# One GpSimd form for the gated inputs, whole-chunk loads, and a new issue order in a gated linear recurrence kernel

## The chip, the core and the metric

The kernel runs on one core of a Trainium2 chip. The metric is the device time of one execution in microseconds (us). The core has a matrix engine (PE, with its weight loads listed apart as PEld), a vector engine (DVE), a scalar engine (ACT), GpSimd (POOL) and SyncE (SP); here SP issues nearly all transfers between DRAM and the on-chip memory SBUF, and 16 DMA engines carry them. Matrix results land in PSUM. Each engine works through its own instructions in order and waits for the others through semaphores.

## What is computed

The inputs x, r_gate and i_gate have shape (4, 6336, 256) in float32. A gated linear recurrence over time is followed by a gated linear unit with a causal convolution of five taps:

```python
log_a = 8.0 * sigmoid(r_gate) * log(clip(sigmoid(a_param), 1e-6, 1 - 1e-6))
a_t = exp(log_a)
x_gated = sqrt(max(1 - a_t * a_t, 1e-6)) * sigmoid(i_gate) * x
for t in range(S):
    h = a_t[:, t] * h + x_gated[:, t]
    y[:, t] = h
gate = sigmoid(sum_k conv_w[k] * y[:, t - 4 + k])
out = (gate * (y @ w_val)) @ w_out
```

Three arrays are read and one is written, 26 MB each.

## The kernel before

The 4 x 6336 tokens are laid end to end (25344 tokens) and cut into 28 chunks (`CHUNKS`, line 16): 256, 512, then 23 of 1024, then 512, 256, 256. A chunk of 1024 is the unit of most counts below; all chunks together are 24.75 such units. Within a chunk, halves of 512 tokens (`subs`) serve as the unit of the later steps. Tokens arrive with time spread over partitions and the 256 channels along the free axis; the recurrence needs channels on partitions and time along the free axis, so the data pass through PE transposes.

The steps of chunk c, by the names that the plan uses:

- `ldri`, `ldx` (lines 216 to 227, SP): load r and i into a slot of `ri` (3 slots, `NRI`), and x into a slot of `xr` (3 slots, `NX`). One transfer for each half chunk and array: 512 KB, in pieces of 4 KB.
- `tanh` (line 293, ACT): tanh of r/2 and i/2, in place.
- `srT` (PE, line 306), `exp` (ACT, line 316): transpose tanh(r/2), and take the exponential into `aring`, which is a_t.
- `e` (POOL, line 322): a_t squared, into `ering`.
- `sq` (ACT, line 368): half the square root of 1 - a_t squared, for up to three chunks in one instruction, written as bf16 over the same ring. ACT loads another function table before it and after it.
- `s1` (POOL, line 336): tanh(i/2) + 1. `u` (POOL, line 359; DVE, line 356, in chunks 0 to 3): that times x, into `uring` (4 slots) in bf16. Two neighbouring tokens of a partition are stored as a pair for each channel, so that a pair can be transposed as one 32-bit value.
- `nT` (PE, line 381): transposes the square roots back, pairs as 32-bit values. `xg` (DVE, line 388): the product of u and nT. `xgT` (PE, line 397): transposes the product, so that time runs along the free axis.
- `scan` (DVE, line 410): the recurrence, in order from chunk to chunk.
- `conv` (PE, line 422), `tg` (ACT, line 433), `val` (PE, line 441), `gv` (DVE, line 447), `out` (PE, line 457), `osbD` or `osbA` (copy out of PSUM by DVE, line 467, or ACT, line 469), `store` (SP, line 480): the gated linear unit and the stores, 512 tokens at a time.

The list `FORM` (line 18) picks one of three forms for `tanh`, `s1` and `u` in each chunk:

- **Form 1** (chunks 4 to 8 and 17 to 27): two `tanh` instructions, the one for i written as float32 in place; `s1` in float32; `u` reads its two inputs with the pair innermost, that is, jumping by 256 elements and back, and writes in order.
- **Form 2** (chunks 0 to 3, on DVE, and 9 to 12): one `tanh` for r and i, written as bf16; `s1` in bf16; `u` reads both inputs in order and writes every second element.
- **Form 3** (chunks 13 to 16): as form 2, but `s1` writes the pairs, and `u` reads x jumping.

The order of all instructions on all engines is the text `PLAN` (lines 34 to 120), written out by hand: one word for each step, chunk, half and PSUM bank. Each engine runs its own share of it in this order. SP too is one queue: a load that waits for its slot holds back the stores behind it, and a store that waits for its copy holds back the loads. A load of r waits until `srT` has read the slot's chunk before it (three chunks earlier), a load of i and of x until `u` has.

Of the kernel before, what the change touches and what calls it, by code (L numbers as in the profile page):

```python
# [8 lines left out]
P = 128  # L9
HP = 64  # L10
SUBN = 512
BANK = 512
# [5 lines left out]
FORM = [2, 2, 2, 2, 1, 1, 1, 1, 1, 2, 2, 2, 2, 3, 3, 3, 3, 1, 1, 1, 1, 1, 1, 1, 1, 1, 1, 1]  # L18
NRI = 3
NX = 3  # L20
# [16 lines left out]
nT.0.0.0 xg.0.0.-1 u.1.-1 xgT.0.0.1 xgT.0.1.0 ldri.3.-1 scan.0.0.-1 scan.0.1.-1 sq.1.1.-1 srT.2.0.1 u.2.-1 srT.2.1.0  # L37
conv.0.0.2 val.0.0.4 exp.2.0.-1 nT.1.0.6 xg.1.0.-1 ldri.4.-1 xgT.1.0.7 xgT.1.1.6 scan.1.0.-1 exp.2.1.-1 e.2.0.-1
scan.1.1.-1 tanh.3.-1 e.2.1.-1 ldri.5.-1 tg.0.0.-1 srT.3.0.1 srT.3.1.0 gv.0.0.-1 exp.3.0.-1 conv.1.0.2 exp.3.1.-1
e.3.0.-1 out.0.0.4 val.1.0.6 tanh.4.-1 osbD.0.0.-1 e.3.1.-1 store.0.0.-1 ldx.3.-1 sq.2.2.-1 srT.4.0.1 s1.4.-1  # L40
srT.4.1.0 ldx.4.-1 u.3.-1 ldx.5.-1 tanh.5.-1 nT.2.0.4 nT.2.1.5 xg.2.0.-1 u.4.-1 xg.2.1.-1 nT.3.0.4 ldri.6.-1 xgT.2.0.5
xg.3.0.-1 scan.2.0.-1 xgT.2.1.4 exp.4.0.-1 scan.2.1.-1 nT.3.1.5 s1.5.-1 exp.4.1.-1 srT.5.0.1 exp.5.0.-1 srT.5.1.0
xg.3.1.-1 ldri.7.-1 e.4.0.-1 exp.5.1.-1 xgT.3.0.1 xgT.3.1.4 scan.3.0.-1 tg.1.0.-1 u.5.-1 tanh.6.-1 conv.2.0.2
gv.1.0.-1 scan.3.1.-1 val.2.0.0 ldx.6.-1 out.1.0.6 tg.2.0.-1 e.4.1.-1 srT.6.0.5 osbD.1.0.-1 srT.6.1.4 tanh.7.-1
conv.2.1.2 ldri.8.-1 e.5.0.-1 gv.2.0.-1 out.2.0.0 e.5.1.-1 val.2.1.6 osbD.2.0.-1 tg.2.1.-1 exp.6.0.-1 s1.6.-1
gv.2.1.-1 conv.3.0.0 exp.6.1.-1 srT.7.0.2 store.1.0.-1 val.3.0.6 e.6.0.-1 tg.3.0.-1 srT.7.1.3 store.2.0.-1 exp.7.0.-1
gv.3.0.-1 conv.3.1.0 e.6.1.-1 exp.7.1.-1 ldx.7.-1 out.2.1.4 tg.3.1.-1 val.3.1.2 osbD.2.1.-1 u.6.-1 sq.4.3.-1 out.3.0.0
gv.3.1.-1 ldx.8.-1 osbD.3.0.-1 out.3.1.2 osbD.3.1.-1 store.2.1.-1 e.7.0.-1 store.3.0.-1 e.7.1.-1 ldri.9.-1 tanh.8.-1
nT.4.0.0 nT.4.1.1 xg.4.0.-1 nT.5.0.2 s1.7.-1 xg.4.1.-1 nT.5.1.3 nT.6.0.0 xg.5.0.-1 xgT.4.0.1 xg.5.1.-1 xgT.4.1.2
xg.6.0.-1 u.7.-1 xgT.5.0.3 scan.4.0.-1 xgT.5.1.4 nT.6.1.5 store.3.1.-1 srT.8.0.0 srT.8.1.6 exp.8.0.-1 xg.6.1.-1  # L50
ldx.9.-1 scan.4.1.-1 xgT.6.0.5 exp.8.1.-1 xgT.6.1.1 s1.8.-1 tanh.9.-1 scan.5.0.-1 ldri.10.-1 conv.4.0.6 e.8.0.-1
scan.5.1.-1 val.4.0.2 u.8.-1 tg.4.0.-1 srT.9.0.0 srT.9.1.6 exp.9.0.-1 gv.4.0.-1 exp.9.1.-1 ldx.10.-1 scan.6.0.-1
conv.4.1.2 e.8.1.-1 out.4.0.6 tg.4.1.-1 scan.6.1.-1 val.4.1.4 tanh.10.-1 ldri.11.-1 e.9.0.-1 conv.5.0.2 gv.4.1.-1
e.9.1.-1 osbD.4.0.-1 out.4.1.0 tg.5.0.-1 val.5.0.4 osbD.4.1.-1 s1.9.-1 sq.7.3.-1 srT.10.0.2 store.4.0.-1 gv.5.0.-1
conv.5.1.6 s1.10.-1 srT.10.1.3 store.4.1.-1 val.5.1.0 ldx.11.-1 out.5.0.4 u.9.-1 osbD.5.0.-1 store.5.0.-1 tg.5.1.-1
nT.7.0.4 nT.7.1.5 xg.7.0.-1 u.10.-1 xg.7.1.-1 ldri.12.-1 nT.8.0.4 exp.10.0.-1 xgT.7.0.5 gv.5.1.-1 conv.6.0.6
exp.10.1.-1 xg.8.0.-1 out.5.1.0 scan.7.0.-1 tg.6.0.-1 val.6.0.2 tanh.11.-1 e.10.0.-1 xgT.7.1.4 gv.6.0.-1 conv.6.1.6
ldri.13.-1 osbD.5.1.-1 nT.8.1.5 e.10.1.-1 val.6.1.2 xg.8.1.-1 tg.6.1.-1 out.6.0.0 scan.7.1.-1 s1.11.-1 tanh.12.-1
srT.11.0.5 srT.11.1.6 xgT.8.0.7 gv.6.1.-1 xgT.8.1.4 u.11.-1 store.5.1.-1 osbD.6.0.-1 conv.7.0.2 exp.11.0.-1
scan.8.0.-1 store.6.0.-1 out.6.1.0 tg.7.0.-1 srT.12.0.5 ldx.12.-1 exp.11.1.-1 val.7.0.2 osbD.6.1.-1 e.11.0.-1  # L60
exp.12.0.-1 nT.9.0.7 srT.12.1.6 gv.7.0.-1 conv.7.1.0 tanh.13.-1 store.6.1.-1 e.11.1.-1 xg.9.0.-1 out.7.0.2 scan.8.1.-1
ldri.14.-1 nT.9.1.7 e.12.0.-1 xg.9.1.-1 tg.7.1.-1 val.7.1.4 osbD.7.0.-1 s1.12.-1 exp.12.1.-1 srT.13.0.7 conv.8.0.0
gv.7.1.-1 exp.13.0.-1 srT.13.1.2 e.12.1.-1 tg.8.0.-1 val.8.0.4 store.7.0.-1 exp.13.1.-1 out.7.1.6 gv.8.0.-1 u.12.-1
ldx.13.-1 sq.10.3.-1 conv.8.1.0 osbD.7.1.-1 out.8.0.2 val.8.1.4 osbD.8.0.-1 store.7.1.-1 xgT.9.0.6 xgT.9.1.7 e.13.0.-1
scan.9.0.-1 store.8.0.-1 ldri.15.-1 e.13.1.-1 scan.9.1.-1 tg.8.1.-1 nT.10.0.2 nT.10.1.3 s1.13.-1 nT.11.0.6 xg.10.0.-1
nT.11.1.7 tanh.14.-1 xg.10.1.-1 conv.9.0.0 gv.8.1.-1 u.13.-1 xgT.10.0.2 xg.11.0.-1 xgT.10.1.3 ldx.14.-1 val.9.0.4
xg.11.1.-1 scan.10.0.-1 out.8.1.6 tg.9.0.-1 tanh.15.-1 ldx.15.-1 conv.9.1.0 gv.9.0.-1 s1.14.-1 srT.14.0.2 osbD.8.1.-1
val.9.1.4 ldri.16.-1 u.14.-1 scan.10.1.-1 srT.14.1.6 tg.9.1.-1 xgT.11.0.7 exp.14.0.-1 out.9.0.0 gv.9.1.-1 exp.14.1.-1
xgT.11.1.3 srT.15.0.2 osbD.9.0.-1 conv.10.0.4 exp.15.0.-1 e.14.0.-1 scan.11.0.-1 srT.15.1.0 tg.10.0.-1 nT.12.0.1
store.8.1.-1 nT.12.1.2 exp.15.1.-1 e.14.1.-1 val.10.0.4 store.9.0.-1 xg.12.0.-1 out.9.1.6 tanh.16.-1 xg.12.1.-1  # L70
gv.10.0.-1 ldri.17.-1 e.15.0.-1 conv.10.1.0 osbD.9.1.-1 out.10.0.4 e.15.1.-1 scan.11.1.-1 xgT.12.0.2 tg.10.1.-1
val.10.1.6 srT.16.0.0 s1.15.-1 sq.13.3.-1 xgT.12.1.1 gv.10.1.-1 srT.16.1.3 store.9.1.-1 osbD.10.0.-1 conv.11.0.6
s1.16.-1 scan.12.0.-1 ldx.16.-1 out.10.1.4 u.15.-1 osbD.10.1.-1 store.10.0.-1 scan.12.1.-1 val.11.0.4 tg.11.0.-1
store.10.1.-1 nT.13.0.2 ldx.17.-1 u.16.-1 xg.13.0.-1 nT.13.1.1 tanh.17.-1 nT.14.0.2 xg.13.1.-1 conv.11.1.6 gv.11.0.-1
xgT.13.0.1 xg.14.0.-1 ldri.18.-1 val.11.1.4 scan.13.0.-1 xgT.13.1.2 tg.11.1.-1 s1.17.-1 exp.16.0.-1 scan.13.1.-1
conv.12.0.6 exp.16.1.-1 e.16.0.-1 out.11.0.0 tg.12.0.-1 gv.11.1.-1 srT.17.0.3 ldri.19.-1 srT.17.1.2 exp.17.0.-1
e.16.1.-1 nT.14.1.6 osbD.11.0.-1 val.12.0.4 exp.17.1.-1 xg.14.1.-1 out.11.1.0 u.17.-1 gv.12.0.-1 tanh.18.-1
conv.12.1.2 osbD.11.1.-1 out.12.0.4 val.12.1.0 store.11.0.-1 osbD.12.0.-1 xgT.14.0.7 tg.12.1.-1 srT.18.0.6 e.17.0.-1
store.11.1.-1 scan.14.0.-1 srT.18.1.4 exp.18.0.-1 conv.13.0.2 store.12.0.-1 exp.18.1.-1 e.17.1.-1 xgT.14.1.5
gv.12.1.-1 nT.15.0.6 ldri.20.-1 tg.13.0.-1 nT.15.1.4 xg.15.0.-1 val.13.0.0 tanh.19.-1 e.18.0.-1 xg.15.1.-1 out.12.1.2  # L80
scan.14.1.-1 conv.13.1.6 e.18.1.-1 xgT.15.0.4 gv.13.0.-1 xgT.15.1.5 tg.13.1.-1 s1.18.-1 osbD.12.1.-1 ldx.18.-1
val.13.1.0 sq.16.3.-1 out.13.0.6 scan.15.0.-1 s1.19.-1 conv.14.0.2 store.12.1.-1 gv.13.1.-1 srT.19.0.4 ldx.19.-1
osbD.13.0.-1 out.13.1.0 u.18.-1 scan.15.1.-1 val.14.0.6 store.13.0.-1 tg.14.0.-1 osbD.13.1.-1 srT.19.1.5 ldx.20.-1
u.19.-1 nT.16.0.0 exp.19.0.-1 gv.14.0.-1 conv.14.1.2 tanh.20.-1 xg.16.0.-1 out.14.0.6 store.13.1.-1 val.14.1.0
osbD.14.0.-1 ldri.21.-1 nT.16.1.4 e.19.0.-1 nT.17.0.6 xg.16.1.-1 nT.17.1.7 tg.14.1.-1 xg.17.0.-1 srT.20.0.4 xg.17.1.-1
exp.19.1.-1 xgT.16.0.6 s1.20.-1 gv.14.1.-1 conv.15.0.2 exp.20.0.-1 scan.16.0.-1 srT.20.1.5 val.15.0.0 tg.15.0.-1
e.19.1.-1 store.14.0.-1 exp.20.1.-1 xgT.16.1.4 out.14.1.2 gv.15.0.-1 ldri.22.-1 u.20.-1 conv.15.1.6 tanh.21.-1
osbD.14.1.-1 out.15.0.0 scan.16.1.-1 val.15.1.2 xgT.17.0.5 osbD.15.0.-1 xgT.17.1.4 tg.15.1.-1 e.20.0.-1 scan.17.0.-1
srT.21.0.0 store.14.1.-1 conv.16.0.6 exp.21.0.-1 e.20.1.-1 store.15.0.-1 srT.21.1.1 tg.16.0.-1 gv.15.1.-1 nT.18.0.0
nT.18.1.5 ldri.23.-1 exp.21.1.-1 e.21.0.-1 xg.18.0.-1 val.16.0.2 xg.18.1.-1 tanh.22.-1 out.15.1.0 scan.17.1.-1  # L90
e.21.1.-1 conv.16.1.6 xgT.18.0.5 gv.16.0.-1 s1.21.-1 xgT.18.1.4 tg.16.1.-1 osbD.15.1.-1 val.16.1.2 ldx.21.-1
sq.19.3.-1 s1.22.-1 out.16.0.6 scan.18.0.-1 conv.17.0.0 store.15.1.-1 gv.16.1.-1 srT.22.0.5 osbD.16.0.-1 ldx.22.-1
val.17.0.2 u.21.-1 scan.18.1.-1 out.16.1.6 store.16.0.-1 tg.17.0.-1 osbD.16.1.-1 srT.22.1.4 ldx.23.-1 nT.19.0.6
u.22.-1 nT.19.1.7 tanh.23.-1 gv.17.0.-1 conv.17.1.0 xg.19.0.-1 out.17.0.2 store.16.1.-1 xg.19.1.-1 nT.20.0.6
# [48 lines left out]
def kernel(  # L143
# [60 lines left out]
    with tc.manual_schedule():  # L204
# [11 lines left out]
        def op_ldri(k, bank):  # L216
            c = k[0]
            for o, n in subs[c]:
                j0, j1 = o // P, (o + n) // P
                for e, src in ((0, rf), (1, if_)):  # L220
                    nc.sync.dma_start(ri[:, c % NRI, e, j0:j1, :], toks(src, c, o, n))  # L221
# [304 lines left out]
```

## Time and profile before

The time before is 348.25 us, the median of 3 runs (347.41 to 348.39). The profiled execution took 345.86 us, of which the span, from the first to the last recorded instruction, is 344.0 us.

| | before |
|---|---|
| median of the runs | 348.25 us |
| profiled execution | 345.86 us |
| its span | 344.0 us |
| bytes moved by the SP queue | 104.35 MB |
| granted TensorE clock, mean | 0.907 |
| last load issued | 296 us |
| last `u` ends on POOL | 312.5 us |

Two kinds of view carry the reading. The first page gives the busy time of each engine, as a sum and in 40 slices of 8.6 us, a digit being tenths of the slice. The view by stretches gives, for any stretch of the span, the busy time of each engine, the granted clock, the share of the DMA engines' time that was used, and what they moved. A share over the whole span says little here, because the first 40 us, the middle and the last 40 us have different limits.

### The profile page before, as it was taken

What the parts mean: (1) busy time and instruction counts of PE and PEld (TensorE: products, weight loads), DVE (VectorE), ACT (ScalarE), POOL (GpSimd) and SP (SyncE); (2) the same over time, 40 slices, a digit from 0 to 9 for tenths busy, and PEclk for the clock granted to TensorE, in tenths of its full rate; (3) what the DMA queues carried; (4) which work ended last, traced back from release to release, by engine and by line L of the source; (5) the groups of instructions that cost most, each with busy time, mean ns of one, the idle gap of its engine ahead of it and who ended that gap; (6) DMA issues with size and microseconds to landing.
All of it is one profiled execution on the core that took longest, in us unless ns stands there. A gap on an engine that the chain in (4) does not pass through costs nothing.

```text
span 344.0 us, 6490 instructions
## 1 busy us (share of the span) xinstructions
PE 258.7 (75%) x2591; PEld 175.1 (51%) x2591; DVE 256.7 (75%) x231; ACT 285.1 (83%) x206; POOL 276.3 (80%) x116
## 2 busy tenths in 40 slices
PE   1157477848576598969968996998479929799994
PEld 0144354548333366646646664765356614565562
DVE  3184478648771699799999998999459934699973
ACT  7999999977737999999999989999597919667553
POOL 1325399999999999899999999999999999952000
PEclk9996879967898899989999999999769976899998
DMA  8999899796798999999999999995999815332334
GB/s 286 370 394 382 338 372 361 242 416 240 272 317 283 362 363 354 403 381 403 381 358 386 392 374 378 324 361 178 368 365 347 345 64 202 136 126 109 138 124 183
DMA packets 30012, 104.76 MB, mean 305 GB/s; under 512 B 3351, under 2 KB 3870, under 8 KB 29982
## 3 DMA queue, kind: packets, MB, share of 16 engines
q1 hardware_dynamic: 29968, 104.35, 81.0%
q8 instruction: 20, 0.33, 0.4%
q14 instruction: 10, 0.08, 0.1%
q10 hardware_dynamic: 14, 0.01, 0.0%
HBM read 78.39 MB, written 25.95 MB: 303 GB/s over the span
## 4 chain that ended last, share of the span: by engine, by line
PE 24%; POOL 20%; DMA 19%; issue 16%; DVE 9%; ACT 7%; SPq 3%; DVEq 0%; POOLq 0%; ACTq 0%
POOL uring L359 12%; PE pp L422 8%; DMA ri<-in_i_gate_dram 7%; PE pp L457 6%; POOL ering L322 6%; PE pp L441 5%; DMA xr<-in_x_dram 5%; DMA ri<-in_r_gate_dram 4%; DVE yring L410 3%; DVE osb L467 3%; POOL ri L336 3%; PE pp L306 2%; ACT tg L433 2%; SPq L221 2%; PE pp L397 2%
## 5 line engine op out<-in xcount | busy, mean ns | idle before, releaser
L359 POOL TENSOR_TENSOR uring<-ri,xr 128x2048 bf16<-128x2048 f32 (+3 forms) x24 | 138.7, 5789 | 7.6 <-PE pp L381 5.0
L410 DVE TENSOR_TENSOR_SCAN yring<-aring,yring,pp 128x1024 bf16<-128x1024 f32 (+2 forms) x54 | 114.8, 2140 | 5.6 <-PE pp L397 4.1
L322 POOL TENSOR_TENSOR ering<-aring 128x1024 f32<-128x1024 f32 (+2 forms) x56 | 93.9, 1701 | 26.6 <-ACT aring L316 26.6
L447 DVE SCALAR_TENSOR_TENSOR gv<-tg,pp 128x1024 bf16<-128x1024 bf16 (+1 forms) x51 | 59.9, 1175 | 29.0 <-ACT tg L433 16.5
L422 PE MATMUL pp<-yring,diag 64*64 64x512 bf16 (+15 forms) x1196 | 72.1, 373 | 8.3 <-ACT tg L433 6.1
L316 ACT ACTIVATE aring<-pp,khf 128x1024 f32<-128x1024 bf16 (+2 forms) x56 | 59.8, 1112 | 5.7 <-PE pp L306 5.7
L441 PE MATMUL pp<-yring,wv 128*128 128x512 bf16 (+1 forms) x204 | 52.5, 380 | 12.9 <-ACT osb L469 6.8
L467 DVE COPY osb<-pp 128x1024 f32<-128x1024 f32 (+1 forms) x39 | 46.3, 1189 | 19.8 <-PE pp L457 17.4
L433 ACT ACTIVATE tg<-pp 128x1024 bf16<-128x1024 f32 (+1 forms) x51 | 51.0, 1000 | 12.0 <-PE pp L422 12.0
L457 PE MATMUL pp<-wo,gv 128*128 128x256 bf16 x396 | 54.4, 282 | 3.6 <-DVE gv L447 3.3
L381 PE MATMUL pp<-ident_f,ering 128*128 128x128 f32 x198 | 37.2, 332 | 25.8 <-ACT ering L368 14.4
L368 ACT ACTIVATE ering<-ering,b 128x4096 bf16<-128x4096 f32 (+4 forms) x16 | 46.7, 2934 | 10.9 <-POOL ering L322 10.7
L457 PEld LDWEIGHTS <-gv 128*128 128x128 bf16 x396 | 41.9, 116 | 21.4 <-DVE gv L447 8.5
L306 PE MATMUL pp<-ident_b,ri 128*128 128x128 bf16 x396 | 33.2, 235 | 22.0 <-ACT ri L301 10.7
L422 PEld LDWEIGHTS <-diag 64*64 64x64 bf16 x1196 | 31.9, 113 | 34.6 <-issue 21.0
L381 PEld LDWEIGHTS pp<-ident_f,ering 128*128 128x128 f32 x198 | 30.4, 211 | 30.9 <-ACT ering L368 15.5
L301 ACT ACTIVATE ri<-ri 128x4096 bf16<-128x4096 f32 (+2 forms) x12 | 39.1, 3261 | 8.1 <-DMA ri<-in_i_gate_dram 8.1
L336 POOL TENSOR_SCALAR ri<-ri 128x2048 f32<-128x2048 f32 (+3 forms) x24 | 44.6, 1870 | 1.0 <-ACT ri L299 1.0
L306 PEld LDWEIGHTS <-ri 128*128 128x128 bf16 x396 | 27.9, 106 | 31.3 <-ACT ri L301 16.6
L388 DVE TENSOR_TENSOR uring<-uring,pp 128x1024 bf16<-128x1024 bf16 (+1 forms) x51 | 33.0, 665 | 11.0 <-PE pp L381 9.5
L397 PE MATMUL pp<-ident_f,uring 128*128 128x128 f32 x198 | 33.7, 304 | 5.7 <-DVE uring L388 4.5
L299 ACT ACTIVATE ri<-ri 128x2048 f32<-128x2048 f32 (+2 forms) x16 | 27.2, 1699 | 9.2 <-DMA ri<-in_i_gate_dram 9.1
(37 smaller groups left out, 132.2 us busy)
## 6 DMA issues: line engine op xcount, KB each, us to landing
ri<-in_r_gate_dram SPq DMA_DIRECT2D x48, 512.0 KB, 7.1
ri<-in_i_gate_dram SPq DMA_DIRECT2D x48, 512.0 KB, 6.7
xr<-in_x_dram SPq DMA_DIRECT2D x48, 512.0 KB, 7.8
out_dram<-osb SPq DMA_DIRECT2D x48, 512.0 KB, 5.2
ri<-in_r_gate_dram SPq DMA_DIRECT2D x3, 256.0 KB, 3.5
ri<-in_i_gate_dram SPq DMA_DIRECT2D x3, 256.0 KB, 2.9
xr<-in_x_dram SPq DMA_DIRECT2D x3, 256.0 KB, 3.5
out_dram<-osb SPq DMA_DIRECT2D x3, 256.0 KB, 2.4
```

What stands on the lines that cost most here:

```text
L306: nc.tensor.transpose(out=ppb[:, bank * 2 * BANK + j * P:bank * 2 * BANK + (j + 1) * P], in_=tri[:, c % NRI, 0, j * D + h * P:j * D + (h + ...
L316: nc.scalar.activation(out=dst, in_=src, func=ACT.Exp, scale=khf[:, h:h + 1], bias=khf[:, h:h + 1])
L322: nc.gpsimd.tensor_tensor(out=ering[:, c % NE, h * n:(h + 1) * n], in0=a, in1=a, op=ALU.mult)
L359: nc.gpsimd.tensor_tensor(out=u, in0=t, in1=xt, op=ALU.mult)
L381: nc.tensor.transpose(out=pp[:, d0:d0 + P], in_=src[:, w, :], identity=ident_f[:])
L410: nc.vector.tensor_tensor_scan(out=yring[:, h, y0:y0 + n], data0=aring[:, c % NA, h, 0:n], data1=src, initial=prev, op0=ALU.mult, op1=ALU.add)
L422: nc.tensor.matmul(out=pp[col * HP:(col + 1) * HP, b0 + d0:b0 + d1], lhsT=diag[r * HP:(r + 1) * HP, h, kk, :], rhs=yring[r * HP:(r + 1) * ...
L433: nc.scalar.activation(out=tg[:, :, 0:n], in_=two(live["conv", k], n), func=ACT.Tanh, scale=0.5)
L441: nc.tensor.matmul(out=pp[:, (bank + m) * BANK:(bank + m) * BANK + n], lhsT=wv[:, hk, m, :], rhs=yring[:, hk, y0:y0 + n], start=(hk == 0), ...
L447: nc.vector.scalar_tensor_tensor(out=gv[:, :, 0:n], in0=live.pop(("tg", k))[:, :, 0:n], scalar=1.0, in1=two(live["val", k], n), op0=ALU.ad ...
L457: nc.tensor.matmul(out=pp[:, bank * BANK + j * D:bank * BANK + (j + 1) * D], lhsT=gv[:, m, 0:n].rearrange("c (p q) -> c q p", q=q)[:, j, : ...
L467: nc.vector.tensor_copy(out=osb[:, 0:w], in_=src)
```

## The change

There are three edits and a new order.

- `FORM` is gone. All chunks use form 2: one `tanh` that writes r and i as bf16, `s1` in bf16, and a `u` that reads in order and writes every second element. Chunks 0 to 3 keep their `u` on DVE.
- A load is one transfer for each array and chunk: 1 MB in pieces of 8 KB for a full chunk.
- With the whole-chunk load, partition p holds 8 neighbouring tokens rather than 4 of each half. The orders in which `exp`, `nT` and `xgT` read and write follow from it: `exp` reads PSUM over 8 blocks; `nT` reads `ering` with a step of 4 values of 32 bits (2 before); `xgT` writes PSUM with a step of 4 (2 before). Stores keep the half chunks and 4 KB pieces.
- `PLAN` is another order of the same 886 steps, from the 24th word on. There are as many steps of each kind as before, the `sq` groups hold the same chunks, and 12 copies are on ACT as before, some of them other ones.

```diff
-FORM = [2, 2, 2, 2, 1, 1, 1, 1, 1, 2, 2, 2, 2, 3, 3, 3, 3, 1, 1, 1, 1, 1, 1, 1, 1, 1, 1, 1]
...
         def op_ldri(k, bank):
             c = k[0]
-            for o, n in subs[c]:
-                j0, j1 = o // P, (o + n) // P
-                for e, src in ((0, rf), (1, if_)):
-                    nc.sync.dma_start(ri[:, c % NRI, e, j0:j1, :], toks(src, c, o, n))
+            for e, src in ((0, rf), (1, if_)):
+                nc.sync.dma_start(ri[:, c % NRI, e, 0:CHUNKS[c] // P, :], toks(src, c, 0, CHUNKS[c]))
 
         def op_ldx(k, bank):
             c = k[0]
-            for o, n in subs[c]:
-                j0, j1 = o // P, (o + n) // P
-                nc.sync.dma_start(xr[:, c % NX, j0:j1, :], toks(xf, c, o, n))
+            nc.sync.dma_start(xr[:, c % NX, 0:CHUNKS[c] // P, :], toks(xf, c, 0, CHUNKS[c]))
...
-            if FORM[c] == 1:
-                nc.scalar.activation(out=tri[:, c % NRI, 0, 0:w], in_=src[:, 0], func=ACT.Tanh, scale=0.5)
-                nc.scalar.activation(out=src[:, 1], in_=src[:, 1], func=ACT.Tanh, scale=0.5)
-                return
             nc.scalar.activation(out=tri[:, c % NRI, :, 0:w], in_=src, func=ACT.Tanh, scale=0.5)
...
-            q = subs[c][0][1] // P
-            src = ppb[:, b * 2 * BANK:b * 2 * BANK + n].rearrange("c (s q p) -> c s p q", p=P, q=q)
-            dst = aring[:, c % NA, h, 0:n].rearrange("c (s p q) -> c s p q", p=P, q=q)
+            src = ppb[:, b * 2 * BANK:b * 2 * BANK + n].rearrange("c (q p) -> c p q", p=P)
+            dst = aring[:, c % NA, h, 0:n].rearrange("c (p q) -> c p q", p=P)
...
+            t = tri[:, c % NRI, 1, 0:CHUNKS[c] * H]
+            nc.gpsimd.tensor_scalar(out=t, in0=t, scalar1=1.0, scalar2=1.0, op0=ALU.add, op1=ALU.mult)
...
+            u = uring[:, c % NU, 0:w].rearrange("p (w d b) -> p w b d", b=2, d=D)
+            t = tri[:, c % NRI, 1, 0:w].rearrange("p (w b d) -> p w b d", b=2, d=D)
+            xt = xr[:, c % NX, 0:w // D, :].rearrange("p (w b) d -> p w b d", b=2)
...
-                i0 = (h * CHUNKS[c] + o) // 2
-                src = ering[:, c % NE, i0:i0 + n // 2].rearrange("c (p w) -> c w p", w=nw)
-                for w in range(nw):
-                    d0 = bank * BANK + w * D + h * P
+                src = ering[:, c % NE, h * nch // 2:(h + 1) * nch // 2].rearrange("c (p w) -> c w p", p=P)
+                for w in range(w0, w1):
+                    d0 = bank * BANK + (w - w0) * D + h * P
                     nc.tensor.transpose(out=pp[:, d0:d0 + P], in_=src[:, w, :], identity=ident_f[:])
...
-            for o, n in subs[c]:
-                nw = n // (2 * P)
-                u = uring[:, c % NU, o * H:(o + n) * H].bitcast(FP32)
-                dst = pp[:, bank * BANK + o // 2:bank * BANK + (o + n) // 2].rearrange("c (p w) -> c w p", w=nw)
...
+            n = CHUNKS[c]
+            u = uring[:, c % NU, 0:n * H].bitcast(FP32)
+            dst = pp[:, bank * BANK:bank * BANK + n // 2].rearrange("c (p w) -> c w p", p=P)
+            for w in range(n // (2 * P)):
```

## The prediction

> **What bounds the kernel now.** I read the page first. Its busy sums are close together (columns: busy us, share of the span, instructions), so no engine's sum decides. The slices show where each is full.
>
> ```profile
> PE 258.7 (75%) x2591; PEld 175.1 (51%) x2591; DVE 256.7 (75%) x231; ACT 285.1 (83%) x206; POOL 276.3 (80%) x116
> ACT  7999999977737999999999989999597919667553
> POOL 1325399999999999899999999999999999952000
> DMA  8999899796798999999999999995999815332334
> ```
>
> POOL is full from 43 us to 300 us without a gap; ACT and DMA have holes in slices 8 to 12 and after 26. The view by stretches, cut at the `tanh` of chunks 9, 11, 22 and 24, shows what the holes mean (columns: stretch; length; busy us of PE, PEld, DVE, ACT, POOL with counts; granted clock; DMA share; GB/s).
>
> ```profile
> 2.00:87.00 85.00, 51.57 (x443) 37.85 (x443) 50.45 (x67) 76.87 (x56) 56.77 (x26) 0.86 0.93 349
> 87.00:121.00 34.00, 21.30 (x178) 12.49 (x175) 19.58 (x15) 24.09 (x14) 34.00 (x11) 0.85 0.86 307
> 121.00:234.00 113.00, 98.97 (x1104) 68.95 (x1105) 106.03 (x83) 109.02 (x71) 111.36 (x45) 0.98 1.00 374
> 234.00:265.00 31.00, 23.34 (x212) 15.74 (x208) 23.04 (x20) 23.98 (x18) 31.00 (x10) 0.83 0.84 311
> 265.00:303.00 38.00, 28.58 (x275) 17.59 (x268) 24.74 (x19) 26.28 (x25) 38.00 (x17) 0.82 0.49 183
> 303.00:344.00 41.00, 34.95 (x399) 22.44 (x397) 32.62 (x30) 24.43 (x27) 4.51 (x6) 0.97 0.36 142
> ```
>
> From 121 to 234 us everything is full: DMA 1.00, ACT 96.5% (109.0 of 113), DVE 94%. There a faster POOL buys nothing. From 87 to 121 and from 234 to 303, POOL alone is full. The chain of waits and ACT's timeline show how it holds the others up to the end: `u` of chunk 23 (L359) gives its slot back, only then is the load of i for chunk 26 issued, and ACT, in order, stands for it with `sq` of chunks 22 to 24 behind.
>
> ```profile
> 272.90 7.31 POOL uring L359
> 280.23 2.70 DMA ri<-in_i_gate_dram
> 283.01 0.63 ACT L299 ACTIVATE ri<-ri 128x512 f32<-128x512 f32 x1 [5.83 <-DMA ri<-in_i_gate_dram]
> ```
>
> SP's own waits say the same: 90.1 us in 17 waits of a load for `u`.
>
> ```profile
> SPq L221 <- POOL uring L359: 90.1, 17, 9.9
> ```
>
> **POOL's part of the change** has rows, since all three forms run now. By shape (columns: busy, mean ns | idle before), float32 is form 1, bf16 forms 2 and 3 together; the timeline tells these apart (171 and 176 us are form 3, 109 and 113 us form 2, two chunks each).
>
> ```profile
> L359 POOL TENSOR_TENSOR uring<-ri,xr 128x2048 bf16<-128x2048 f32 x13 | 96.8, 7453 | 5.2 <-PE pp L381 5.0
> L359 POOL TENSOR_TENSOR uring<-ri,xr 128x2048 bf16<-128x2048 bf16 x8 | 34.0, 4270 | 0.3
> ...
> L336 POOL TENSOR_SCALAR ri<-ri 128x2048 f32<-128x2048 f32 x13 | 24.7, 1907 | 1.0 <-ACT ri L299 1.0
> ```
>
> ```profile
> 109.67 3.78 POOL L336 TENSOR_SCALAR ri<-ri 128x2048 bf16<-128x2048 bf16 x2
> 113.39 8.20 POOL L359 TENSOR_TENSOR uring<-ri,xr 128x2048 bf16<-128x2048 bf16 x2
> 171.20 5.00 POOL L336 TENSOR_SCALAR ri<-ri 128x2048 bf16<-128x2048 bf16 x2
> 176.09 8.77 POOL L359 TENSOR_TENSOR uring<-ri,xr 128x2048 bf16<-128x2048 bf16 x2
> ```
>
> Form 2 costs 4.12 us for `u` (about half of 8.20) and 1.9 for `s1`, form 1 7.45 and 1.9, form 3 4.4 and 2.5. Going to form 2: 13 x (7.45 - 4.12) = 43.3; the three small chunks, scaled by the same ratio, 3.5 of 7.9; form 3, 4 x (0.3 + 0.6) = 3.6. POOL falls by 50 us, from 276 to about 226. It was full for some 260 us, so it is no longer the bound, and what this is worth is the slack of the next engines.
>
> **ACT.** Form 1's two `tanh` take 2 x 1.913 us, form 2's one 3.618: 13 x 0.21 = 2.7 us less. Against it, the one `tanh` waits for r and i, where r's half could run while i was in flight. L299 waited three times for i, so at most 3 x 1.9 = 5.7 us are lost, at least 0; waits of this kind shrink when slots come free earlier, and I take 0. `exp` with 8 blocks: its times for 256, 512 and 1024 elements are 564, 778 and 1212 ns, a constant slope, although the first has blocks of 2 and the others of 4. I take 0.
>
> **Transfers.** The same bytes, in 84 loads for 153, 69 issues of 0.45 us fewer on SP. SP is not the bound, for it spends its time in waits. Below, a coarser load can land a first half later; above, longer pieces can move more. I take 0. Two statements of the Trainium skill would alter the sum. "DMA: Bandwidth & Descriptors", Anatomy of one DMA, fits a fixed 2.0 us to each transfer (measured on GpSimd's path), and its Bandwidth section counsels 1 MB; 69 x 2.0 would be 138 us gained. That is for transfers one after another; here 512 KB transfers overlap, and 374 GB/s over 113 us at share 1.00 leave no such gaps. The other speaks against the change: its Specifications put HBM for one core at about 358 GB/s. The loads up to chunk 24 (23.75 units x 3.15 MB = 74.7 MB) and the stores of some 18.5 units (19.4 MB) are 94.1 MB; at 358 that is 263 us, and chunk 24's `tanh` is at 265 already: nothing would be left to gain before the tail. The row decides: 374 on average over the full stretch, and as a best stretch
>
> ```profile
> 149.00:161.00 12.00, 11.33 (x102) 8.07 (x103) 10.99 (x10) 11.97 (x8) 11.76 (x6) 0.86 1.02 407
> ```
>
> At 374, 94.1 MB take 252 us.
>
> **PE.** `nT`'s weight load reads every second 32-bit value; `xgT`'s reads in order. Between 186 and 200 us (min/median/max ns):
>
> ```profile
> L381 PEld LDWEIGHTS pp<-ident_f,ering x12: 194/209/216, 188.7 to 198.1; 128*128 128x128 f32 x12
> L397 PEld LDWEIGHTS pp<-ident_f,uring x8: 138/140/143, 194.0 to 197.2; 128*128 128x128 f32 x8
> ```
>
> The step of 2 costs 70 ns of load, yet the matmuls follow each other every 120 ns rather than 109, since loads overlap. The change makes it a step of 4, 16 bytes, for which no row exists. The Trainium skill ("SBUF — State Buffer", Door 1) says SBUF has lines of 16 bytes and needs two hits in a line for full speed; the step of 2 has two hits and was dearer all the same. By line counts (32, 64, 128 in a row of 128 values) the load would go to 140 + 3 x 70 = 350 ns. From the row alone `nT` gains 0; with the rule, a load hidden by half, the pace becomes some 190 ns: 190 transposes x 70 = 13 us of PE, spread over the span, of which I put 1.5 us on the path (in the full tail). `xgT`'s PSUM step doubles to 16 bytes; at 8 bytes it shows no price (109 ns against 120), so 0, at most a doubling to 220.
>
> **The order.** The same steps, so no busy time. I take 0; bound from both sides by 5 us, one of the waits seen (4 to 7 us at 261 to 295 us) gained or lost.
>
> **The sum.** Each stretch shrinks until DMA moves 374 GB/s or ACT is 96.5% busy, whichever takes longer.
> - 2 to 87: DMA 85 x 349/374 = 79.3, ACT 79.7: -5.3.
> - 87 to 121: DMA 34 x 307/374 = 27.9, ACT 25: -6.1.
> - 121 to 234: ACT's cheaper `tanh` only, DMA holds: -1.
> - 234 to 265: DMA 25.8, ACT 24.9: -5.2.
> - 265 to 303: loads no longer wait for `u`. PE at the 85% of the last stretch: 28.6/0.85 = 33.6; ACT 27.2: -4.4 to -10, I take -7.
> - 303 to 344: PE and DVE with their dependences, POOL idle: 0.
> - PE's dearer transposes: +1.5.
>
> Together -23: span 344 -> 321, execution 345.9 -> 323. The runs' median stood 2.4 us over the profiled execution (0.7%), so 325 by median.
>
> **Rivals.**
> - **A, the sum**: 325 (317 to 332). For it: the holes of ACT and DMA lie where POOL alone is full. 0.58.
> - **B, the hole was not POOL's alone**: DMA gives no more than 358, or SP's stores hold loads back instead (`store` waited 72 and 41 us for copies, 37 of it at the end). Then -2, -5, 0, -4 and -4.4: -15.4 + 1.5 = -14, median 334. Against it: 374 over 113 us. 0.18.
> - **C, PE's strides become the bound; slower.** PE is 258.7 busy and reached 88% in its fullest stretch. If the step of 4 takes both kinds of transposes to 300 ns, PE gains 198 x (180 + 191) = 73 us; 332 at 90% is a span of 369, median 373. It decides from 0.9 x 344 - 258.7 = 51 us on, that is, 129 ns more for each of 396 transposes. Against it: 70 ns of load for the step of 2 gave 11 ns of pace. 0.10.
> - **D, more**: 8 KB pieces move 400 GB/s and ACT packs to 99%: -7, -8, -5, -7, -10 = -37, median 311. 0.11.
> - **No change**: form 2 costs more in other company. Eight neighbours at 4.1 to 4.4 speak against it. 0.03.
>
> **Range and chances.** From D's edge to past B: 309 to 338; C is left out, and the far ends of D and B. A measurement of this kernel tells 0.3% (1 us) from no change. Faster: A, B, D, 0.87; same 0.03; slower 0.10.
>
> **What would show it.** `u` at 4.1 us in all chunks, POOL near 226 us with idle time before `u`; SP's wait for `u` far below 90 us; DMA share near 1.00 until chunk 24, whose `tanh` comes near 247 us; `nT`'s load at 209 to 350 ns. Wrong, if DMA's share stays under 0.95 although SP doesn't wait for POOL, if PE's pace in L381 or L397 passes 240 ns, or if waits for stores take POOL's place.

## The result, and the profile after

The changed kernel takes 321.14 us (median of 4 runs, 320.46 to 323.72) where the one before took 348.07 beside it: a ratio of 0.924, with a 95% interval of 0.919 to 0.930. The forecast was 325, with 309 to 338 around it. The profiled execution took 321.38 us, its span is 319.6. Medians and ratios, here and below, leave out executions in a slower state, more than 1.5% above the fastest of the same kernel.

The page of the kernel after, its busy sums and the slices of POOL, DMA and the granted clock (8 us each):

```profile
PE 246.9 (77%) x2591; PEld 171.1 (54%) x2591; DVE 257.7 (81%) x231; ACT 283.0 (89%) x190; POOL 227.4 (71%) x116
POOL 0215478996999969957997699995995999561000
PEclk9998958998999799998999999999999999999999
DMA  7999999099999979989999989999999897613343
GB/s 223 398 385 421 419 425 403 23 325 425 424 412 371 362 292 326 410 331 388 366 337 385 414 308 392 346 385 424 398 349 391 317 351 270 249 72 131 134 180 150
```

POOL fell from 276.3 to 227.4 us and now has gaps all along. ACT, with 89% of the span, is the fullest. One slice stands out, the eighth: 56 to 64 us, in which the DMA engines moved 23 GB/s. A second profile of the same kernel has the hole in the same slice, with 20 GB/s.

POOL's rows by shape (columns: busy, mean ns | idle before and what ended it), and SP's own waits:

```profile
L333 POOL TENSOR_TENSOR uring<-ri,xr 128x2048 bf16<-128x2048 bf16 x21 | 86.4, 4120 | 14.0 <-DMA xr<-in_x_dram 11.1 <-PE pp L370 2.5
L320 POOL TENSOR_SCALAR ri<-ri 128x2048 bf16<-128x2048 bf16 x21 | 39.7, 1902 | 7.1 <-ACT ri L292 7.1
```

```profile
SPq L453 <- DVE osb L440: 164.7, 37, 14.6
SPq L453 <- ACT osb L442: 33.8, 12, 5.0
SPq L218 <- PE pp L297: 14.4, 3, 7.9
SPq L218 <- POOL uring L333: 10.2, 5, 4.2
```

The waits of stores before:

```profile
SPq L480 <- DVE osb L467: 72.1, 25, 8.3
SPq L480 <- ACT osb L469: 41.4, 12, 7.3
```

`u` on POOL takes 4.12 us in every full chunk, and three times it waited for x, 11.1 us in all. SP's waits of loads of r and i for POOL's `u` shrank from 90.1 us to 10.2; those of stores for their copies grew from 72.1 + 41.4 to 164.7 + 33.8.

The view by stretches, cut at the `tanh` of the same chunks as the prediction (9, 11, 22, 24), so that the lengths of the rows can be laid beside it:

```profile
2.00:90.00 88.00, 49.85 (x459) 36.11 (x459) 52.17 (x67) 77.91 (x53) 55.48 (x29) 0.90 0.92 361
90.00:114.00 24.00, 17.76 (x170) 11.45 (x163) 18.83 (x15) 23.21 (x14) 23.41 (x10) 0.93 0.96 378
114.00:229.00 115.00, 101.77 (x1119) 70.94 (x1121) 108.78 (x85) 107.34 (x65) 98.07 (x46) 0.99 0.96 367
229.00:252.00 23.00, 18.95 (x194) 13.54 (x187) 21.00 (x18) 22.89 (x14) 19.74 (x10) 1.00 0.97 364
252.00:319.60 67.60, 58.61 (x663) 39.04 (x661) 56.72 (x48) 51.28 (x48) 30.02 (x20) 1.00 0.53 197
```

The total agrees with the sum, but the parts do not: the first stretch took 88 us where 79.7 were expected and 85 were taken before. The cut moves with the order, though: by the `tanh` of chunk 9 PE has done 459 matmuls here and 443 before. That asked for experiments which take form, loads and order apart.

### The profile page after: what moved, and what is told of

It reads as the page before. It is cut to its first block, busy times and chain, and to the rows that moved or that the text cites. A ratio compares the mean times of both kernels' runs of the same rounds, so it can differ in the third digit from the quotient of the medians.

```text
span 319.6 us, 6375 instructions
## 1 busy us (share of the span) xinstructions
PE 246.9 (77%) x2591; PEld 171.1 (54%) x2591; DVE 257.7 (81%) x231; ACT 283.0 (89%) x190; POOL 227.4 (71%) x116
## 4 chain that ended last, share of the span: by engine, by line
PE 21%; ACT 17%; POOL 15%; issue 14%; DVE 11%; DMA 11%; SPq 0%; POOLq 0%; DVEq 0%; ACTq 0%
DMA ri<-in_i_gate_dram 8%; PE pp L395 7%; POOL ering L312 6%; POOL uring L333 6%; DVE yring L383 5%; ACT ering L342 5%; PE pp L430 5%; PE pp L414 4%; ACT ri L292 4%; ACT tg L406 3%; DVE gv L420 3%; DMA xr<-in_x_dram 3%; DVE osb L440 2%; PE pp L355 2%; ACT L342 2%
## 5 line engine op out<-in xcount | busy, mean ns | idle before, releaser
L333 POOL TENSOR_TENSOR uring<-ri,xr 128x2048 bf16<-128x2048 bf16 (+2 forms) x24 | 90.8, 3792 | 14.1 <-DMA xr<-in_x_dram 11.1
L292 ACT ACTIVATE ri<-ri 128x4096 bf16<-128x4096 f32 (+2 forms) x28 | 90.1, 3223 | 7.2 <-DMA ri<-in_i_gate_dram 4.4
L395 PE MATMUL pp<-yring,diag 64*64 64x512 bf16 (+14 forms) x1196 | 67.3, 350 | 5.8 <-ACT tg L406 3.4
L430 PE MATMUL pp<-wo,gv 128*128 128x256 bf16 x396 | 53.4, 278 | 11.6 <-DVE gv L420 11.1
L414 PE MATMUL pp<-yring,wv 128*128 128x512 bf16 (+1 forms) x204 | 51.5, 375 | 4.2 <-DVE osb L440 4.0
L355 PE MATMUL pp<-ident_f,ering 128*128 128x128 f32 x198 | 36.2, 323 | 18.4 <-ACT ering L342 11.1
L320 POOL TENSOR_SCALAR ri<-ri 128x2048 bf16<-128x2048 bf16 (+2 forms) x24 | 42.0, 1760 | 10.9 <-ACT ri L292 10.8
L297 PE MATMUL pp<-ident_b,ri 128*128 128x128 bf16 x396 | 30.7, 229 | 17.6 <-ACT ri L292 15.9
L355 PEld LDWEIGHTS pp<-ident_f,ering 128*128 128x128 f32 x198 | 29.6, 210 | 26.0 <-ACT ering L342 14.6
L297 PEld LDWEIGHTS <-ri 128*128 128x128 bf16 x396 | 25.8, 103 | 26.2 <-ACT ri L292 19.8
L370 PE MATMUL pp<-ident_f,uring 128*128 128x128 f32 x198 | 32.2, 292 | 8.1 <-DVE uring L362 6.8
L370 PEld LDWEIGHTS pp<-ident_f,uring 128*128 128x128 f32 x198 | 24.1, 148 | 18.8 <-issue 9.9
```

The source lines that it names most:

```text
L292: nc.scalar.activation(out=tri[:, c % NRI, :, 0:w], in_=src, func=ACT.Tanh, scale=0.5)
L333: nc.gpsimd.tensor_tensor(out=u, in0=t, in1=xt, op=ALU.mult)
L355: nc.tensor.transpose(out=pp[:, d0:d0 + P], in_=src[:, w, :], identity=ident_f[:])
L395: nc.tensor.matmul(out=pp[col * HP:(col + 1) * HP, b0 + d0:b0 + d1], lhsT=diag[r * HP:(r + 1) * HP, h, kk, :], rhs=yring[r * HP:(r + 1) * ...
L414: nc.tensor.matmul(out=pp[:, (bank + m) * BANK:(bank + m) * BANK + n], lhsT=wv[:, hk, m, :], rhs=yring[:, hk, y0:y0 + n], start=(hk == 0), ...
L430: nc.tensor.matmul(out=pp[:, bank * BANK + j * D:bank * BANK + (j + 1) * D], lhsT=gv[:, m, 0:n].rearrange("c (p q) -> c q p", q=q)[:, j, : ...
```

## The experiments

The theory was that **form 2** is all of the gain, through POOL. Its rivals: the **loads** (longer transfers move more), and the **order** (the steps stand better for the new lengths). Each experiment was timed beside the kernel before on its own chip; the ratios refer to that.

### The edits one by one

Form 2 alone, in the kernel before:

```diff
-FORM = [2, 2, 2, 2, 1, 1, 1, 1, 1, 2, 2, 2, 2, 3, 3, 3, 3, 1, 1, 1, 1, 1, 1, 1, 1, 1, 1, 1]
+FORM = [2] * 28
```

> The kernel before with form 2 in all chunks, and nothing else: its half-chunk loads and its order stay. Theory form (POOL's 50 us are the cause): most of the 27 us, 322 to 332 us, POOL near 226 us busy, SP's wait for u far below 90 us. Theory order (the old order was made for other lengths and wastes what is freed): 335 to 345 us. Theory loads (longer transfers are the cause): 340 us or more.

Measured: 318.2 us, 0.917 (0.913 to 0.920). One line of the diff gives the whole gain, and more than the 322 to 332 us expected. POOL's busy time is 226.6 us, SP's wait for `u` 17.3 us. ACT, with 16 instructions fewer, falls only from 285.1 to 282.6 us.

The loads alone (whole-chunk transfers and the layout that follows, with the old forms and the old order; of the edit only the load of x is shown):

```diff
...
-            for o, n in subs[c]:
-                j0, j1 = o // P, (o + n) // P
-                nc.sync.dma_start(xr[:, c % NX, j0:j1, :], toks(xf, c, o, n))
+            nc.sync.dma_start(xr[:, c % NX, 0:CHUNKS[c] // P, :], toks(xf, c, 0, CHUNKS[c]))
...
```

> The kernel before with whole-chunk loads in 8 KB pieces and the layout that follows from them; the mixed forms and the old order stay. Theory form: no gain, 345 to 351 us, POOL stays at 276 us. Theory loads: 325 to 335 us, since DMA moves more in the same time. Theory order: 345 us or more.

Measured: 346.3 us, 0.998 (0.996 to 1.001). Nothing, and POOL stays at 276.4 us.

Form 2 and the loads, in the old order (the edit is the old `PLAN` in the changed kernel):

> The changed kernel with the order of the kernel before: form 2 and whole-chunk loads, old order. Theory form: within 4 us of form 2 alone, 320 to 330 us. Theory loads: clearly below form 2 alone. Theory order: 335 us or more, so that the new order is worth 14 us or more.

Measured: 317.9 us, 0.916 (0.913 to 0.919), level with form 2 alone. So the loads give nothing with form 2 either.

The loads and the new order, with the mixed forms (the edit is the old `FORM`, with the branches that belong to it, in the changed kernel):

> The changed kernel with the mixed forms of the kernel before: whole-chunk loads and the new order, POOL as slow as it was. Theory form: 343 to 352 us. Theories order and loads: 330 us or less.

Measured: 346.1 us, 0.997 (0.994 to 1.000). Without form 2, loads and order together gain about 0.3%, at most 0.6%; against the loads alone (346.3 us) the new order gains nothing.

### Is the new order dearer?

The changed kernel and form 2 alone were run again, side by side.

> The changed kernel itself, once more, beside form 2 alone on the same chip. Form 2 alone gave 318.2 us, this one 321.1 in its own measurement. If the new order costs something: 2 to 4 us above form 2 alone. If the difference was between chips: within 1 us of it.

> Form 2 alone in the kernel before (half-chunk loads, old order), the same kernel as the first experiment, to be compared with the changed kernel on one chip. 316 to 319 us; 2 to 4 us below the changed kernel if the new order costs something, level with it if not.

Measured: 320.8 us, 0.921 (0.916 to 0.927), against 317.5 us, 0.913 (0.909 to 0.917). The intervals just touch. Together with the earlier measurements (0.924 against 0.917 and 0.916 for the two kernels in the old order), the new order most likely costs 0.8 to 0.9%, some 3 us. Form 2 in the old order, 317.5 to 318.2 us with either kind of load, is the fastest of all kernels here.

The stretches tell where to look. First form 2 alone, then form 2 with whole-chunk loads in the old order, which differs from the changed kernel in `PLAN` alone (both cut at the `tanh` of the same chunks):

```profile
2.00:83.00 81.00, 47.11 (x408) 33.96 (x409) 47.78 (x66) 76.54 (x52) 51.72 (x28) 0.92 1.00 376
83.00:109.00 26.00, 19.77 (x210) 11.98 (x210) 21.69 (x16) 23.60 (x14) 26.00 (x11) 0.93 1.00 384
109.00:219.00 110.00, 95.14 (x1081) 66.72 (x1079) 103.95 (x82) 106.57 (x65) 100.18 (x46) 1.00 0.99 382
219.00:243.00 24.00, 20.47 (x206) 14.22 (x205) 22.84 (x20) 23.54 (x15) 20.36 (x9) 1.00 1.00 380
243.00:314.20 71.20, 61.71 (x694) 40.43 (x692) 59.32 (x49) 51.94 (x48) 27.62 (x19) 0.99 0.48 184
```

```profile
2.00:83.00 81.00, 49.77 (x407) 35.71 (x407) 47.12 (x66) 75.85 (x51) 51.52 (x27) 0.92 0.97 376
83.00:109.00 26.00, 19.63 (x218) 12.30 (x217) 21.69 (x16) 24.94 (x16) 25.73 (x12) 1.00 0.96 379
109.00:219.00 110.00, 94.79 (x1070) 66.66 (x1069) 103.69 (x81) 105.12 (x63) 99.24 (x46) 0.98 0.99 383
219.00:243.00 24.00, 20.48 (x206) 14.21 (x206) 22.83 (x20) 23.62 (x15) 21.01 (x10) 1.00 0.96 374
243.00:314.60 71.60, 62.43 (x698) 40.83 (x696) 60.12 (x50) 52.52 (x49) 28.43 (x19) 1.00 0.48 186
```

With the same loads, DMA moves 374 to 383 GB/s up to chunk 24 in the old order and 361 to 378 in the new one. DMA's share says less: with whole-chunk loads it is 0.96 to 0.99 in the old order too. The first stretch takes 81 us against 88, in part because more work stands before the cut (459 matmuls against 407). SP's timeline of the changed kernel in that stretch (start, us busy, line, operation):

```profile
42.97 0.33 SPq L218 DMA_DIRECT2D ri<-in_r_gate_dram  x1
47.17 0.33 SPq L218 DMA_DIRECT2D ri<-in_i_gate_dram  x1
47.55 15.96 SPq L453 DMA_DIRECT2D out_dram<-osb  x3
63.61 0.37 SPq L218 DMA_DIRECT2D ri<-in_r_gate_dram  x1
64.08 0.74 SPq L218 DMA_DIRECT2D ri<-in_i_gate_dram  x1
```

The new order puts the stores of chunks 0 and 1 and of chunk 2's first half ahead of the loads of r and i for chunk 8. SP stands there for a copy (14.6 us of wait in one piece) until 63.6 us, and the loads in flight run dry: this is the hole in the DMA slice. The copy itself is late because DVE runs four scans (9.1 us, from 50.6) before it. The `u` that frees the slot of i (chunk 5) had ended at 59.3. The load of x for chunk 7 stood behind these stores too: its slot was free from 47.1 us, when `u` of chunk 4 ended, and it was issued at 67.1. In the old order SP issues loads of r, i and x all through 48 to 57 us, and from 56 to 64 us DMA moves 403 GB/s (form 2 with whole-chunk loads) where it moves 20 here.

The hole is not the only loss in this stretch. ACT's timeline of the changed kernel, before the hole, and the `tanh` of chunk 4 in form 2 with whole-chunk loads in the old order:

```profile
33.75 1.02 ACT L406 ACTIVATE tg<-pp 128x1024 bf16<-128x1024 f32 x1 [3.57 <-PE pp L395]
37.35 3.61 ACT L292 ACTIVATE ri<-ri 128x4096 bf16<-128x4096 f32 x1
```

```profile
32.41 3.61 ACT L292 ACTIVATE ri<-ri 128x4096 bf16<-128x4096 f32 x1
```

The new order puts `tg` of chunk 1 ahead of the `tanh` of chunk 4, and ACT stands 3.57 us for its convolution (4.07 in the second profile). That `tanh` starts 4.9 us later than in the old order, before any hole. Of the ACT time that the new order loses in the first stretch (10.1 us idle against 5.2), 3.9 us lie before 36 us. So there are two candidates, the hole and this wait. An order with the one store behind the load, or with `tg` moved back, was not tried, and which of them costs the 3 us stays open.

### SP's queue sorted

If stores ahead of loads are harmful, an SP queue sorted by readiness should help in the old order too. The loads of r and i became steps of their own, and SP's words in `PLAN` alone were moved, on top of form 2, whole-chunk loads and the old order:

```diff
...
-        def op_ldri(k, bank):
+        def op_ldr(k, bank):
...
+        def op_ldi(k, bank):
...
```

> Form 2 and whole-chunk loads in the old order, with SP's queue alone sorted by when each load and store could start (loads of r and i as steps of their own); all other engines keep their order. In the old SP order, loads stood some 500 us in sum behind something else. If that holds DMA back: 310 to 315 us. If DMA is full in any case: level with 318 us. Rival: stores and loads in order of readiness crowd out the loads that ACT needs next, 319 to 325 us.

Measured: 318.8 us, 0.917 (0.912 to 0.922): level. SP's waits with the same loads in the old SP order, then in the sorted one (line numbers differ):

```profile
SPq L453 <- DVE osb L440: 140.5, 37, 10.1
SPq L218 <- PE pp L297: 6.8, 4, 3.0
```

```profile
SPq L448 <- DVE osb L435: 96.1, 29, 7.9
SPq L209 <- PE pp L292: 56.0, 20, 7.9
```

The sort exchanged waits and did not shorten them: those for DVE's copies fell from 140.5 us to 96.1, those for `srT` on PE rose from 6.8 to 56.0, and all of SP's waits together are 248.5 us before and 251.4 after. DMA moved 380 to 386 GB/s up to 240 us, about as much as in the old SP order. So the run does not show what fewer waits would be worth. The sum of SP's waits says little in any case: form 2 alone has 205.5 us of them and, with whole-chunk loads, 248.5, at the same 318 us. That a wait costs time where what is in flight runs out, as in the hole above, fits this but was not tested. (No view shows the 500 us of the expectation.)

### Which engine binds, by doses

POOL, by other work than `u`, in the changed kernel:

```diff
             nc.gpsimd.tensor_tensor(out=ering[:, c % NE, h * n:(h + 1) * n], in0=a, in1=a, op=ALU.mult)
+            if h == 1:
+                nc.gpsimd.tensor_tensor(out=ering[:, c % NE, h * n:(h + 1) * n], in0=a, in1=a, op=ALU.mult)
```

> The changed kernel with each chunk's second squaring on POOL (e, half 1) done twice: 24.75 units x 1.9 = 47 us more on POOL, 227 to 274 us, the output unchanged. Theory form, by POOL's sum: the old time comes back, 340 to 350 us, by whatever work POOL is filled. Rival, it was u's form itself (its reads in the way of other engines, the slot of r and i held in float32): below 332 us.

Measured: 338.7 us, 0.974 (0.968 to 0.979). In its profile, POOL's busy time is 274.4 us, and `u` is unchanged:

```profile
PE 250.9 (75%) x2591; PEld 173.6 (52%) x2591; DVE 257.7 (77%) x231; ACT 283.7 (85%) x190; POOL 274.4 (82%) x144
POOL 1426799999999999999999999999999999774000
...
L335 POOL TENSOR_TENSOR uring<-ri,xr 128x2048 bf16<-128x2048 bf16 x21 | 86.2, 4117 | 0.6
```

The result lies between the two expectations, with the interval (336.8 to 340.6 us) just reaching the first. Filling POOL with a squaring makes it full again from 42 to 284 us and costs 18.0 us on the 320.8, but the mixed forms in the same order cost 25.4 us (346.1) at nearly the same POOL time (277.4 us). So some 70% of the price of the mixed forms comes back with POOL's time alone, by other work. The rest is open. One difference is how it lies: the dose adds 1.9 us to each full chunk and delays what `sq` waits for, while form 1 adds 3.3 us to 13 chunks and delays what frees the slots. ACT also has 1.5 us more to do with the mixed forms (285.2 against 283.7).

ACT, in the changed kernel:

```diff
             nc.scalar.activation(out=dst, in_=src, func=ACT.Exp, scale=khf[:, h:h + 1], bias=khf[:, h:h + 1])
+            if h == 1:
+                nc.scalar.activation(out=dst, in_=src, func=ACT.Exp, scale=khf[:, h:h + 1], bias=khf[:, h:h + 1])
```

> The changed kernel with each chunk's second exponential on ACT done twice: 24.75 x 1.2 = 29 us more on ACT, 283 to 312 us, the output unchanged. If ACT is what binds now: 15 to 25 us more, 336 to 346 us (the first stretches and the middle at full price, the tail at a part). If DMA binds and ACT has slack: less than 8 us more.

Measured: 334.3 us, 0.962 (0.958 to 0.967). That is 13.5 us more than 320.8, for 29.1 us of work (ACT 283.0 -> 312.1 us busy, 94% of its span): between the two expectations, nearer the first. ACT is close to binding but still had slack: its idle time fell from 36.6 to 20.7 us of the span, so about half of the dose went into it.

DMA, in the changed kernel, by loading half of x a second time:

```diff
             nc.sync.dma_start(xr[:, c % NX, 0:CHUNKS[c] // P, :], toks(xf, c, 0, CHUNKS[c]))
+            if CHUNKS[c] == CMAX:
+                nc.sync.dma_start(xr[:, c % NX, 0:4, :], toks(xf, c, 0, CMAX)[:, 0:4, :])
```

> The changed kernel with the first half of x loaded a second time in each full chunk: 23 x 0.52 = 12.1 MB more, at 374 GB/s 32 us of all DMA engines, the output unchanged. If DMA binds: 20 to 30 us more, 341 to 351 us. If ACT binds and DMA follows it: less than 10 us more.

Measured: 407.9 us, 1.173 (1.167 to 1.179), 87 us more, far over the full price of 32. The experiment measured something else, as SP's waits show:

```profile
SPq L224 <- DMA xr<-in_x_dram: 237.3, 23, 15.8
```

The second load writes where the first one does, so SP waits until that has landed, with all loads and stores behind it. The dose says nothing on the bytes, so whether DMA or ACT binds in the changed kernel was not settled by it. It does show what a stock of loads in flight is worth: 23 waits of some 10 us for a landing, with the bytes, cost 87 us.

### Early and late chunks

The prediction's sum gave the gain to stretches. Form 2 in some of the chunks only, in the kernel before:

```diff
-FORM = [2, 2, 2, 2, 1, 1, 1, 1, 1, 2, 2, 2, 2, 3, 3, 3, 3, 1, 1, 1, 1, 1, 1, 1, 1, 1, 1, 1]
+FORM = [2, 2, 2, 2, 2, 2, 2, 2, 2, 2, 2, 2, 2, 3, 3, 3, 3, 1, 1, 1, 1, 1, 1, 1, 1, 1, 1, 1]
```

> The kernel before with form 2 in chunks 4 to 8 too; chunks 17 to 27 stay in form 1, 13 to 16 in form 3. My sum by stretches gives these chunks the gain before 121 us: 11 us, 335 to 339 us. Rival, POOL's time counts wherever it is freed: 5 x 3.33 = 17 us of the 50, so 17/50 of the gain of 29, 10 us, 337 us; the two agree here. Rival, the middle gives it back, being full: no gain, 345 us or more.

Measured: 333.5 us, 0.958 (0.952 to 0.964), 14.6 us less than the 348.0 beside it.

```diff
-FORM = [2, 2, 2, 2, 1, 1, 1, 1, 1, 2, 2, 2, 2, 3, 3, 3, 3, 1, 1, 1, 1, 1, 1, 1, 1, 1, 1, 1]
+FORM = [2, 2, 2, 2, 1, 1, 1, 1, 1, 2, 2, 2, 2, 3, 3, 3, 3, 2, 2, 2, 2, 2, 2, 2, 2, 2, 2, 2]
```

> The kernel before with form 2 in chunks 17 to 27 too; chunks 4 to 8 stay in form 1, 13 to 16 in form 3. My sum by stretches gives these chunks the gain from 190 us on: 13 to 14 us, 333 to 335 us. Rival, POOL's time counts wherever it is freed: 30 of the 50 us, so 17 us of 29, 330 us or less.

Measured: 331.5 us, 0.952 (0.945 to 0.959), 16.6 us less.

Each part gives some 3 us more than my sum. Early, the result (interval 331 to 336 us) is below both the sum (335 to 339) and its rival (337), and that the middle gives it back is refuted. Late, the result lies between the sum (333 to 335) and the rival (330 or less), and the interval, 329 to 334 us, reaches both, so this run alone decides nothing. The two add up to 31.1 us, and form 2 in all chunks gave 30.4 in its second measurement (317.5 against 347.9): what is freed early is not given back in the full middle. Taken together they speak against POOL's time counting alike wherever it is freed: 16.6 us freed early gave 14.6, the 30.1 us freed late (8 x 3.33 + 3.5) gave 16.6.

## Why the prediction was right

The mechanism held: POOL was the bound outside the full middle, and form 2 lifts it. That the number came within 4 us is in part luck, for two misses pull apart. For form 2 in the old order, which the sum describes, 325 was 7 us too slow (318.2), and the new order, taken at nothing, costs some 3.

**POOL.** `u` at 4.12 us in all chunks, 226 us in sum: measured 4.120 and 227.4. That one form is the cause was the main point, and form 2 alone confirms it: 318.2 us, with nothing left for loads and order.

**The sum by stretches** was made for form 2 with the order at nothing, so the kernel to lay beside it is form 2 in the old order. The price of the transposes, 1.5 us, was put in the tail.

| stretch | before | predicted | form 2, old order | after |
|---|---|---|---|---|
| 2 us to chunk 9 | 85 | 79.7 | 81 | 88 |
| chunk 9 to 11 | 34 | 27.9 | 26 | 24 |
| chunk 11 to 22 | 113 | 112 | 110 | 115 |
| chunk 22 to 24 | 31 | 25.8 | 24 | 23 |
| chunk 24 to the end | 79 | 73.5 | 71.2 | 67.6 |
| span | 344 | 321 | 314.2 | 319.6 |

The method holds for that kernel, 1 to 3 us off in each row. A second profile of it gives 80.8, 25.2, 113.2, 25.4 and 70.5 us, so a row is good to some 3 us only. In the changed kernel the sum is right in the total and wrong in the first stretch by 8 us, part of which is the moved cut; the tail and the second stretch give back 5.9 and 3.9.

**The order** was the mis-sized term: taken at 0 within 5 us. It costs about 3 us, within the bound, probably in places that I had not looked at: three stores ahead of loads in SP's queue at 47 us, and ACT's wait for a convolution at 30 us. I had read SP's waits in the old order only, as sums, and not walked the new order of the words against the time at which each input would be ready.

**The DMA ceiling.** The row decided against the lower figure, rightly: form 2 in the old order moved 376 to 384 GB/s at shares of 0.99 to 1.00 from 2 to 243 us (380 on average, 377 in its second profile), against 374 in the sum and 358 by the Trainium skill ("DMA: Bandwidth & Descriptors", Specifications). The 1 to 2% above the 374 would alone take 2 to 4 us off these 241, about half of what the sum left out. The first half of rival B, which stood on the lower figure, falls. Its other half, SP's stores holding loads back, is what the hole at 56 to 64 us shows in the changed kernel; its price was not separated.

**The signs of being wrong.** Two of those named did appear in the changed kernel. DMA's share was 0.92 in the first stretch although SP waited for POOL's `u` only 10.2 us in the whole run, and waits of stores grew from 113.5 to 198.5 us while those for `u` fell from 90.1. The second was a poor sign: form 2 with whole-chunk loads in the old order has 184.7 us of such waits and is among the fastest.

**The transfers' size** at nothing: 346.3 against 347.0 with the old forms, 317.9 against 318.2 with form 2. DMA's share of 0.96 to 1.00 up to chunk 24 in both kernels with form 2 fits the reason given, that transfers overlap. Rival D, 400 GB/s by longer pieces, did not come: up to chunk 24 the changed kernel moved 361 to 378.

**ACT.** 2.7 us less from `tanh` was expected; the whole engine fell by 2.1, with another order of table loads and copies around it. The single `tanh` that waits for both loads cost nothing to be seen: ACT's waits for i fell from 17.2 us (9.1 and 8.1) to 4.4.

**PE.** `nT` reads and `xgT` writes with a step of 16 bytes now. The weight loads of `nT` and `xgT` in the changed kernel (min/median/max ns):

```profile
L355 PEld LDWEIGHTS pp<-ident_f,ering x198: 138/209/231, 15.1 to 295.8; 128*128 128x128 f32 x198
L370 PEld LDWEIGHTS pp<-ident_f,uring x198: 137/140/230, 21.3 to 309.3; 128*128 128x128 f32 x198
```

`nT`'s median is 209 ns, as with a step of 8 bytes, and the mean matmul of `nT` and of `xgT` did not lengthen (323 and 292 ns, before 332 and 304). The estimate of 350 ns by lines of 16 bytes ("SBUF — State Buffer", Door 1, in the Trainium skill) did not come true, and my 1.5 us and rival C fall with it.

**The tail.** 7 us were expected from loads that no longer wait for `u`; 7.8 came in the old order, 11.4 in the new one.

## What to carry to other kernels

Time freed on a full engine is worth, stretch by stretch, what the next engine there leaves: here 50 us of POOL gave 30, nearly all of it early and half of it late. When an order is rewritten along with a faster step, run the faster step in the old order first; here that was the better kernel, by some 3 us. In one in-order queue of loads and stores, the sum of the queue's waits told little here (205.5 and 248.5 us at the same time); a hole in the DMA row, and the first long idle piece of the fullest engine, showed where to look.

## What the runs showed of the hardware

- A product of 2048 elements on GpSimd takes 7.45 us when float32 inputs are read jumping by 1 KB and back, and 4.12 us when bf16 and float32 inputs are read in order and the bf16 output is written with a step of 4 bytes. Type and order of the inputs change together here and were not taken apart. A jumping write of `s1` costs 2.5 us against 1.9. Where one operand must jump, here it was cheaper for `u` to jump in its write: `s1` and `u` take 6.0 us together in form 2 and 6.9 in form 3.
- A PE weight load of 128 x 128 float32 takes 138 to 140 ns from values in order and 209 ns from values with a step of 8 or of 16 bytes.
- The mean granted TensorE clock was 0.893 to 0.936 in the runs of the kernel before, 0.947 to 0.968 in those of the changed one, 0.945 to 0.971 with form 2 alone, and 0.859 to 0.867 in the kernel of 408 us. So it does not rank the last few us: form 2 alone is faster than the changed kernel at the same clock. PE's busy time fell from 258.7 to 246.9 us with the same 2591 matmuls. What moves the clock was not tried.
